# Retention with a gated MLP: the order in which the second tile's outputs and chunk 21 are made, and a queue for one early load

## Chip, cores, metric

The kernel runs on one core of one Trainium2 chip. The metric is the device time of one execution in microseconds; three runs of the kernel before gave 298.43 (median), 298.27 and 302.54. The engines are named as the profile names them: PE is TensorE, DVE is VectorE, ACT is ScalarE, POOL is GpSimd, SP is SyncE, which issues DMA transfers; PEld is TensorE's weight load.

## What is computed

The inputs are q, k and v of 8 batches, 8 heads, 576 positions and 64 columns, and two weights. Everything is given in float32.

```python
scores = (1/sqrt(64)) * q @ k.T                   # per batch and head
gamma  = 1 - 2 ** (-5 - head)
Dmat   = gamma ** (i - j) where i >= j, else 0
attn   = (scores * Dmat) @ v                      # a decaying, causal, linear attention
x      = attn with the heads side by side         # 4608 rows of 512
h      = x @ w_in                                 # 512 -> 2048
g      = h * tanh(softplus(h))                    # mish
out    = g @ w_out                                # 2048 -> 512
```

## The kernel before

**Chunks and tiles.** A chunk is 128 rows of the attention (all heads of 128 positions). There are 36. Chunks 0 to 7 are the first 128 positions of the eight batches. From chunk 8 on, two batches follow each other: three chunks each, and then one chunk that holds the last 64 positions of both. Chunk 14 is the first of these last ones, chunk 21 the second. Four chunks make a tile of 512 rows for the products of the MLP, so there are nine tiles: tile 0 is chunks 0 to 3, tile 1 is chunks 4 to 7.

**The products.** `g1(t, f)` makes 128 of the 2048 hidden columns of tile t: four matmuls of 128x512 into a bank `hp`, then mish on ScalarE into `gT`. `g2(t, i)` makes a quarter of the sum for one of the tile's four output chunks: four matmuls into a bank `ops`. The fourth quarter is followed by a copy (`res`) and a store. Both issue their matmuls in `product` (L527, or L532 where a matmul is cut in two halves of 256 columns).

**The attention of a first chunk** (tiles 0 and 1) is direct. `f_transpose` makes q and k transposed, `f_scores` the masked scores `sm0`, `f_v` the values in bf16 (`vb`), and `f_out` the outputs: eight matmuls (L249) of `vb` with `sm0` into a bank, and a copy to `xT`, the tile's input for `g1`. For tile 1 two calls share one `sc` tile, which has two banks: b = 0 and 2 take its first bank, b = 1 and 3 the second. There the copy stands behind the second call of each pair and moves both halves.

**The other chunks** keep a running state. A chunk n is loaded by POOL's queue (`load`: q and k into `qkraw`, v into `vraw`), scaled by VectorE with two instructions (`step_p`, L304, into `qks`), transposed (`step_t`: before chunk 16 on TensorE, from 16 on by a DMA transpose on SP's queue, L333, held behind a matmul, its gate), and worked on two at a time in a `visit`: states (L402), outputs (L461, L478), scores of the next two (L347), then the copies of the outputs to `xT` (L490, one on ScalarE, one on VectorE) and the masked scores `sm` (L353, VectorE). The banks of the visit's outputs are two `hp`, the same that `g1` needs next. `hold` makes POOL's queue wait for a transposed chunk before it goes on with loads.

**Order.** Everything is ordered by hand: each engine works its instructions in the order in which the program lists them, and waits at semaphores. The scheduler only places the waits. A wait is placed by tile and buffer. The stretches that matter here are:

- The start: two loads of f32 q for batches 0 and 1 into `q0` (L121, on SP's queue), loads of k, q, v and weights on POOL's queue, and VectorE's cast of `q0` to bf16 (L639).
- The loop over the 16 columns blocks i of tile 0's second product (`g2_first(i // 4, i % 4)`, L696 to L711). The table `steps` (L695) says which work of tile 1 stands ahead of which block. "V0" to "V3" are the calls of `f_v`, "O0" to "O3" those of `f_out`. The blocks 12 to 15 are the last quarters of tile 0's four output chunks, each followed by its copy and store, by VectorE for even and ScalarE for odd chunks.
- The loop from L776 on, over tiles t and steps i. n counts the chunk that is visited next, w = i % 8 the step in its eighth; the visit of n and n + 1 stands at w = 6. At w = 4 and 5 or 4 and 7 (L797) the two chunks n + 4 and n + 5 are scaled, and their transposes stand at w = 6 and 7 (L800, L826, L837 to L839). `NPE` is 18. At n = 16, w = 5, VectorE also has `f_state` (L803, the values `v0s` of a later batch).

So, before, at n = 16: chunk 20 is scaled at w = 4, chunk 21 at w = 5, the visit of 16 and 17 is at w = 6, and both transposes follow it.

Of the kernel before, what the change touches and what calls it, by code (L numbers as in the profile page):

```python
# [16 lines left out]
def kernel(  # L17
# [18 lines left out]
    nc = tc.nc  # L36
    B, H, S, D = q.shape
    assert (B, H, S, D) == (8, 8, 576, 64)
    P = 128
# [6 lines left out]
    NPE = 18  # L46
    NT = 16
# [50 lines left out]
    q0 = gts[0][:, H:nF, :].bitcast(F32).rearrange("p (b a) c -> p b (a c)", a=2)  # L98
    v0 = {}
    fst = {}  # L100
# [17 lines left out]
        nc.gpsimd.dma_start(out=pair, in_=v[ds(b, 2), :, 0:P, :].rearrange("b h p d -> p (b h) d"))  # L118

    for b in range(2):  # L120
        nc.sync.dma_start(out=q0[:, b, :], in_=q[b, :, 0:P, :].rearrange("h (g r) d -> g h (r d)", r=8))  # L121
    for b in range(2):
        load_first_qk(0, 1, b)

# [47 lines left out]
    xts = {}  # L172
# [5 lines left out]
    def f_mix(g, i):  # L178

        name = ("qb", "kb")[i]  # L180
        fst[1][name, "mix", g] = first.tile([P, 8, 2, D], BF16, name=name + "x")
        nc.vector.tensor_copy(fst[1][name, "mix", g].rearrange("p r x d -> p x r d"),
                              fst[1][name][:, ds(2 * g, 2), :].rearrange("p x (r d) -> p x r d", r=8))

    def f_transpose(t, g, i, parts):

        name = ("qb", "kb")[i]
        out_t = tr.tile([P, 2, NP, P], BF16, name="qkT", bufs=6).rearrange("p i n t -> p (i n) t")
        n = 8 // len(parts)
        moves = []  # L190
        for j, (pool, tname, copy) in enumerate(parts):
            tp = pool.tile([P, 2, 8, P] if tname == "sc" else [P, 8, P], BF16, name=tname)
            tp = (tp[:, 0] if tname == "sc" else tp)[:, 0:n]
            for r in range(n):
                if t == 1:
                    mix = fst[1][name, "mix", g][:, n * j + r]
                    nc.tensor.transpose(tp[:, r, :], mix.rearrange("p x d -> p (x d)"), ident)
                else:
                    for x in range(2):
                        nc.tensor.transpose(tp[ds(64 * x, 64), r, :],  # L200
                                            fst[0][name][:, 2 * g + x, ts(n * j + r, D)], ident)
            moves.append((copy, out_t.rearrange("p h (g r) -> p h g r", r=8)[:, :, :, ds(n * j, n)],
                          tp.rearrange("p r (g h) -> p h g r", h=H)))
        for copy, to, src in moves:
            copy(to, src)
        fst[t][name, g] = out_t
# [21 lines left out]
    def f_v(t, b, copy):  # L228
        vb = first.tile([P, H, D], BF16, name="vb", bufs=4)
        copies = copy if isinstance(copy, tuple) else (copy,)  # L230
        n = H // len(copies)
        for j, copy in enumerate(copies):
            copy(vb[:, ds(n * j, n), :], v0[4 * t + b][:, ds(n * j, n), :])
        fst[t]["vb"][b] = vb

    def f_out(t, b, copy):
        if b == 0:
            xts[t] = xp.tile([P, KC, NCH * P], BF16, name="xT")
        vb = fst[t]["vb"][b]
        if t == 0:  # L240
            pool, name = ((ps_h, "hp"), (ps_h, "hp"), (ps_st, "st"), (ps_o, "ops"))[b]
            ot = pool.tile([P, NP, P], F32, name=name)
        else:
            if b % 2 == 0:
                fst[1]["out"] = ps_sc.tile([P, 2, NP, P], F32, name="sc")
            ot = fst[1]["out"][:, b % 2]
        for p in range(NP):
            for e in range(2):
                nc.tensor.matmul(ot[ds(64 * e, 64), p, :], lhsT=vb[:, 2 * p + e, :],  # L249
                                 rhs=fst[t]["sm", b][:, 2 * p + e, :],  # L250
                                 start=(p == 0), stop=True, skip_group_check=True)
        if t == 0:
            copy(xts[t][:, :, ts(b, P)], ot)
        elif b % 2:
            copy(xts[1].rearrange("p h (b i) -> p b h i", i=P)[:, ds(b - 1, 2)], fst[1]["out"])

    def f_state(t, b, engine=nc.gpsimd):

# [187 lines left out]
    def run(jobs, *how):  # L446
        while jobs:
            jobs.pop()(*how)
# [141 lines left out]
    def g2_first(part, s):  # L590

        if part == 0:
            pool, name = ((ps_h, "hp"), (ps_h, "hp"), (ps_o, "ops"), (ps_st, "st"))[s]
            outs[0, s] = pool.tile([P, d_model], F32, name=name)
        for f in range(4 * part, 4 * part + 4):
            halved[0] = 1
            product(outs[0, s], gts[0][:, f, ts(s, P)], w_out_t[:, f, :], f == 0, f == nF - 1)
        if part == 3:
            store(0, s, outs[0, s], nc.scalar.copy if s % 2 else nc.vector.tensor_copy)
# [30 lines left out]
    dve, act, pool = nc.vector.tensor_copy, nc.scalar.copy, nc.gpsimd.tensor_copy  # L630
# [61 lines left out]
        g1(0, f)  # L692
    for i in range(2):
        f_mix(0, i)
    steps = {0: "T0", 3: "S0 C1", 9: "T1", 11: "S1", 12: "V0 V1 V2 V3", 14: "O0 O1", 15: "O2 O3"}  # L695
    for i in range(nF):  # L696
        for step in steps.get(i, "").split():
            n = int(step[1])
            if step[0] == "T":
                for j in range(2):  # L700
                    f_transpose(1, n, j, [(ps_sc, "sc", (dve, act)[j])])
            elif step[0] == "S":
                f_scores(1, n)
            elif step[0] == "V":
                f_v(1, n, dve if n == 3 else act)
            elif step[0] == "C":
                for j in range(2):
                    f_mix(n, j)
            else:
                f_out(1, n, (dve, act)[n // 2])  # L710
        g2_first(i // 4, i % 4)  # L711
    load_k0(1)

# [12 lines left out]
    for u in range(24):  # L726
        j, w = divmod(u, 4)
# [48 lines left out]
    for t in range(2, nT + 1):  # L776
        for i in range(nF):
            n, w = NCH * (t + 1) + i // 8 * 2, i % 8
            if w == 2 and n in cast_at:
                cast_k0(cast_at[n])  # L780
            if w == 2:
                run(casts, act)
                halved[0] = {14: 16, 20: 29}.get(n, 0)
            if w == 6 and n + 4 == NPE:
                load_k0(3)
            if w == 6 and n < n_chunks:
                visit(n, ((ps_h, "hp"), (ps_h, "hp")), (act, dve), lambda: g2(t - 1, i))
            if w == 0:
                stores(act if n == N0 + 4 else dve)
                run(sums)  # L790
            if w == 7 and n + 2 == NPE:
                stores()
            if w in (0, 1) and n + 2 < NT:
                att(n + 2 + w, "P")
            if w in ((3, 4) if n + 2 < NPE else (0, 1)):
                att(n + 2 + (w in (1, 4)), "V")
            if w in ((4, 7) if n + 4 <= NPE else (4, 5)) and n + 4 >= NT:  # L797
                stores()
                att(n + 4 + (w != 4), "P")
            if w == 7 and NT <= n + 4 <= NPE:  # L800
                step_t(n + 5, newest[0])
            if w == 5 and 16 <= n < 24:
                f_state(1, n // 2 - 8, nc.vector)  # L803


            if w in (1, 3) and n + 2 == NT:
                more_loads(n + 5 + w // 3, newest[0])
            if w == 1 and n + 2 == NPE:
                more_loads(n + 5, newest[0])
            if w == 1 and NPE < n + 2 < n_chunks:  # L810
                hold(n + 2)
            if w == 1 and n + 2 >= NPE:
                more_loads(n + 7)
                if t in (3, 4):
                    load_k0(2 * t - 2 + i // 8)
            if w in (4, 5) and n + 2 < NT:
                att(n - 2 + w, "T")
            stores()


            if t == 2:
                if w == 6:
                    g2(1, 8 + i // 2)
                g1(t, i)
                if w == 6:
                    step_t(n + 4, newest[0])  # L826
                if i % 2 and w != 7:
                    g2(1, 8 + i // 2)
            elif t == nT:
                if i < 12:  # L830
                    g2(t - 1, i)
            elif w == 6:

                last = n < n_chunks <= n + 2
                g2(t - 1, i + last)
                g1(t, i)
                if NPE < n + 4 < n_chunks:  # L837
                    for x in (4, 5):
                        step_t(n + x, newest[0])  # L839
            elif w == 7 and n < n_chunks <= n + 2:  # L840
                g1(t, i)
            elif i % 4 == 0:
                g1(t, i)
                g1(t, i + 1)
                g2(t - 1, i)
            else:
                if i % 4 != 1:
                    g1(t, i)
                g2(t - 1, i)
# [32 lines left out]
```

## Time and profile before

| | |
|---|---|
| median of three runs | 298.43 us |
| the profiled execution, its own time | 298.47 us |
| its span, first to last instruction | 296.8 us |
| TensorE (PE) busy | 287.3 us, 97% |
| VectorE (DVE) busy | 138.3 us, 47% |
| ScalarE (ACT) busy | 133.1 us, 45% |
| GpSimd (POOL) busy | 128.0 us, 43% |
| HBM | 38.80 MB read, 9.44 MB written |
| granted TensorE clock | 1.000 over the span |

How to read the lines. A line of the timeline has the start in us, the length in us, the engine, the line of the kernel, the operation, what it writes and reads, the shape, and the number of instructions that are merged in it; in square brackets stand the idle time ahead of it and what ended that. In a wait line, the numbers are the total in us, the number of waits and the longest. Matmuls are pipelined: the length of a row of matmuls holds the drain of the last one, so the next row can begin before it ends, and start-to-start distances are what the work costs. A DMA issue's length is that of the issuing, and the landing is later.

### The profile page before, as it was taken

To read this page: it belongs to the slowest core of one execution; us is meant where nothing else is said; L and a number is where in the kernel's file an instruction comes from. 1 tells how busy PE (TensorE), PEld (TensorE's weight loads), DVE (VectorE), ACT (ScalarE), POOL (GpSimd) and SP (SyncE) were. 2 spreads that over 40 slices of the span, in tenths; PEclk is the share of its full clock that TensorE was granted. 3 is DMA by queue.
4 is the path that set the end of the run, shared out by engine and by line. 5 is a ranking of instruction groups with operands and counts; after the bars stand their busy time and mean duration, and the time that the engine had idled before them with its cause. 6 is when DMAs were issued, how large, how long until landed. Compare 5 with 4: busy or idle time off the path is not lost.

```text
span 296.8 us, 7900 instructions
## 1 busy us (share of the span) xinstructions
PE 287.3 (97%) x3442; PEld 157.1 (53%) x3480; DVE 138.3 (47%) x251; ACT 133.1 (45%) x219; POOL 128.0 (43%) x167
## 2 busy tenths in 40 slices
PE   8899999999999999999999999999999999999996
PEld 3466887555456544457645454545454544444443
DVE  5841646697955828453546453535354222010011
ACT  4866126776665444444363435343434433433200
POOL 8845756666818195557384727283020000000000
PEclk9999999999999999999999999999999999999999
DMA  7999999999989999998979868686314110110131
GB/s 159 223 201 205 205 239 216 339 228 211 258 200 187 178 228 239 176 246 204 201 192 203 207 159 209 145 204 145 83 48 95 38 38 37 37 35 35 53 91 71
DMA packets 42275, 47.97 MB, mean 162 GB/s; under 512 B 23936, under 2 KB 31104, under 8 KB 42240
## 3 DMA queue, kind: packets, MB, share of 16 engines
q0 software_dynamic: 15440, 32.25, 51.4%
q1 hardware_dynamic: 26656, 15.01, 21.3%
q8 instruction: 27, 0.44, 0.7%
q10 hardware_dynamic: 144, 0.20, 0.2%
q14 instruction: 8, 0.07, 0.1%
HBM read 38.80 MB, written 9.44 MB: 163 GB/s over the span
## 4 chain that ended last, share of the span: by engine, by line
PE 78%; DMA 14%; POOL 4%; issue 2%; DVE 2%; DVEq 0%; POOLq 0%
PE hp L527 37%; PE ops L527 29%; DMA vpair<-in_v_dram 4%; DMA w_out_t<-in_moe_w_out_dram 4%; DMA w_in_t<-in_moe_w_in_dram 3%; DMA qkraw<-in_k_dram 2%; PE hp L532 2%; PE ops L532 2%; PE sc L347 1%; PE sc L402 1%; PE hp L478 1%; PE hp L608 1%; PE hp L461 1%; POOL gT L107 1%; PE sc L325 1%
## 5 line engine op out<-in xcount | busy, mean ns | idle before, releaser
L527 PE MATMUL hp<-xT,w_in_t 128*128 128x512 bf16 (+1 forms) x507 | 126.5, 376 | 1.2 <-DVE xT L490 0.4
L564 ACT ACTIVATE gT<-hp 128x512 bf16<-128x512 f32 x142 | 84.8, 598 | 91.1 <-PE hp L527 84.6
L527 PE MATMUL ops<-w_out_t,gT 128*128 128x512 bf16 x411 | 101.9, 379 | 2.0 <-issue 1.9
L527 PEld LDWEIGHTS <-w_in_t 128*128 128x128 bf16 x528 | 51.4, 98 | 53.9 <-issue 0.9
L527 PEld LDWEIGHTS <-gT 128*128 128x128 bf16 x478 | 45.5, 98 | 52.6 <-issue 0.6
L616 DVE COPY res<-ops 128x512 f32<-128x512 f32 x28 | 19.3, 690 | 89.5 <-PE ops L527 89.5
L304 DVE TENSOR_TENSOR qks<-qkraw,gqk 128x512 bf16<-128x512 f32 x56 | 35.3, 683 | 7.3 <-DMA qkraw<-in_k_dram 7.3
L282 POOL DMA_DIRECT2D qkraw<-in_q_dram x24 | 21.5, 896 | 14.5 <-PE hp L527 7.0
L311 POOL TENSOR_TENSOR vs<-vraw,gv 128x512 bf16<-128x512 f32 x16 | 16.4, 1044 | 17.2 <-PE hp L461 17.1
L282 POOL DMA_DIRECT2D vraw<-in_v_dram x24 | 21.4, 893 | 3.1 <-DMA vpair<-in_v_dram 1.5
L282 POOL DMA_DIRECT2D qkraw<-in_k_dram x24 | 21.2, 885 | 2.4 <-DMA qkraw<-in_q_dram 0.9
L490 DVE CAST xT<-hp 128x512 bf16<-128x512 f32 x13 | 9.0, 691 | 27.1 <-PE hp L478 27.1
L490 ACT CAST xT<-hp 128x512 bf16<-128x512 f32 x14 | 8.2, 586 | 28.5 <-PE hp L478 28.5
L532 PEld LDWEIGHTS <-gT 128*128 128x128 bf16 x164 | 15.7, 98 | 3.2
L438 DVE TENSOR_TENSOR total<-sc,total 128x256 f32<-128x256 f32 x40 | 16.9, 421 | 1.0
L496 POOL COPY held<-qkT 128x1 bf16<-128x1 bf16 x8 | 1.5, 189 | 36.6 <-DMA qkT<-qks 36.6
L353 DVE TENSOR_TENSOR sm<-sc,mask 128x1024 bf16<-128x1024 f32 x14 | 17.0, 1215 | 0.3 <-PE sc L347 0.3
L532 PE MATMUL hp<-xT,w_in_t 128*128 128x256 bf16 x102 | 15.7, 272 | 0.0
L532 PEld LDWEIGHTS <-w_in_t 128*128 128x128 bf16 x104 | 10.2, 98 | 6.8 <-issue 0.4
L441 ACT CAST ssb<-total 128x768 bf16<-128x768 f32 (+3 forms) x13 | 11.7, 896 | 1.7 <-DVE total L438 1.6
L527 PE MATMUL hp<-w_out_t,gT 128*128 128x512 bf16 x49 | 12.0, 379 | 0.2 <-issue 0.2
L532 PE MATMUL ops<-w_out_t,gT 128*128 128x256 bf16 x80 | 10.4, 273 | 0.1
(126 smaller groups left out, 251.7 us busy)
## 6 DMA issues: line engine op xcount, KB each, us to landing
out_dram<-res SPq DMA_DIRECT2D x31, 256.0 KB, 3.0
qkraw<-in_q_dram POOLq DMA_DIRECT2D x24, 256.0 KB, 6.4
qkraw<-in_k_dram POOLq DMA_DIRECT2D x24, 256.0 KB, 6.7
vraw<-in_v_dram POOLq DMA_DIRECT2D x24, 256.0 KB, 6.9
w_out_t<-in_moe_w_out_dram POOLq DMA_DIRECT2D x4, 512.0 KB, 11.8
k0r<-in_k_dram POOLq DMA_DIRECT2D x8, 256.0 KB, 7.7
gT<-in_k_dram POOLq DMA_DIRECT2D x8, 128.0 KB, 6.3
gT<-in_v_dram POOLq DMA_DIRECT2D x2, 512.0 KB, 7.4
```

Source lines behind the costliest of these rows:

```text
L107: nc.gpsimd.dma_start(out=fst[t][name][:, b, :], in_=(q, k)[i][4 * t + b, :, 0:P, :].rearrange("h (g r) d -> g h (r d)", r=8))
L282: ins = nc.gpsimd.dma_start(out=t, in_=src[b, :, ds(P * c, P), :].rearrange("h p d -> p h d"))
L304: nc.vector.tensor_tensor(slots[:, :, y], heads[:, :, y], factors[:, :, y].unsqueeze(3).to_broadcast([P, NP, 2, D]), op=OP.mult)
L311: engine.tensor_tensor(vs, live[n]["v"], gv[:, c, :].unsqueeze(2).to_broadcast([P, H, D]), op=OP.mult)
L353: nc.vector.tensor_tensor(sm.rearrange("p e x n i -> p (e x n) i"), live[n]["sc"].rearrange("p e x n i -> p (e x n) i"), mask.unsqueeze(1) ...
L438: nc.vector.tensor_tensor(new[:, k], st[:, j, x], total[b], op=OP.add)
L441: casts.append(lambda copy: copy(lows[:, 0:k], new[:, 0:k]))
L490: copy(xts[t][:, :, ds(P * s, 2 * P)].rearrange("p h (x j i) -> p j h x i", x=2, j=2)[:, j], both[j])
L527: newest[0] = nc.tensor.matmul(to, lhsT=w, rhs=x, start=first, stop=last)
L532: nc.tensor.matmul(to[:, ts(j, n)], lhsT=w, rhs=x[:, ts(j, n)], start=False, stop=False, skip_group_check=True)
L564: done = nc.scalar.activation(gts[t][:, f, :], hp, AX.Mish)
L616: copy(ot, ops)
```

## The change

Three places are changed.

1. *The second tile's outputs.* In the table, O0 and O1 move from ahead of block 14 to ahead of block 15, where O2 and O3 stand. Each call of `f_out` now ends with a copy of its own 512 columns: VectorE for b = 0 and 2, ScalarE for b = 1 and 3. Before, VectorE copied O0 and O1 in one instruction of 1024 columns, and ScalarE O2 and O3. The calls of a pair still share one `sc` tile.
2. *Chunk 21.* At n = 16, w = 4 and 7 are the steps at which the chunks n + 4 and n + 5 are scaled, so chunk 21 is scaled at w = 7, behind the visit at w = 6. Its transpose is issued at w = 7, right behind its scaling, and no longer together with that of chunk 20. On VectorE's queue the two instructions for chunk 21 move past `v0s`, a copy to `xT` and `sm`. On SP's queue the order is the same.
3. *The load of q.* The second of the two f32 loads of q is issued on ScalarE's queue, ahead of its table load, and no longer on SP's.

```diff
-        nc.sync.dma_start(out=q0[:, b, :], in_=q[b, :, 0:P, :].rearrange("h (g r) d -> g h (r d)", r=8))
+        (nc.sync, nc.scalar)[b].dma_start(out=q0[:, b, :], in_=q[b, :, 0:P, :].rearrange("h (g r) d -> g h (r d)", r=8))
...
-        if t == 0:
-            copy(xts[t][:, :, ts(b, P)], ot)
-        elif b % 2:
-            copy(xts[1].rearrange("p h (b i) -> p b h i", i=P)[:, ds(b - 1, 2)], fst[1]["out"])
+        copy(xts[t][:, :, ts(b, P)], ot)
...
-    steps = {0: "T0", 3: "S0 C1", 9: "T1", 11: "S1", 12: "V0 V1 V2 V3", 14: "O0 O1", 15: "O2 O3"}
+    steps = {0: "T0", 3: "S0 C1", 9: "T1", 11: "S1", 12: "V0 V1 V2 V3", 15: "O0 O1 O2 O3"}
...
-                f_out(1, n, (dve, act)[n // 2])
+                f_out(1, n, (dve, act)[n % 2])
...
-            if w in ((4, 7) if n + 4 <= NPE else (4, 5)) and n + 4 >= NT:
+            if w in ((4, 7) if n + 4 <= NPE + 2 else (4, 5)) and n + 4 >= NT:
                 stores()
                 att(n + 4 + (w != 4), "P")
-            if w == 7 and NT <= n + 4 <= NPE:
+            if w == 7 and NT <= n + 4 <= NPE + 2:
                 step_t(n + 5, newest[0])
...
                 if NPE < n + 4 < n_chunks:
-                    for x in (4, 5):
+                    for x in ((4, 5) if n + 4 > NPE + 2 else (4,)):
                         step_t(n + x, newest[0])
```

Lines of the changed kernel are three lower from L255 on, and the copy of `f_out` is its L252.

## The prediction

> **What bounds the kernel now.** I read the page first, then TensorE's waits, then two stretches of the timeline: 43 to 50 us, where the second tile's outputs are made, and 111 to 117 us, where chunk 21 is scaled. From the page:
>
> ```profile
> span 296.8 us, 7900 instructions
> PE 287.3 (97%) x3442; PEld 157.1 (53%) x3480; DVE 138.3 (47%) x251; ACT 133.1 (45%) x219; POOL 128.0 (43%) x167
> ...
> PE 78%; DMA 14%; POOL 4%; issue 2%; DVE 2%; DVEq 0%; POOLq 0%
> ```
>
> TensorE (PE) is busy for 97% of the span and is 78% of the chain that ended last. DMA is 14% of that chain, all but 2% of it before 45.4 us (the weights, then `vpair`); after that the chain is TensorE alone but for one place. So there is almost no idle time in which a later loss could be made good, and every idle moment that a change puts on TensorE is paid in full. Of TensorE's waits, only one after 13 us is not "issue":
>
> ```profile
> PE hp L527 <- DVE xT L490: 0.4, 1, 0.4
> ```
>
> The columns are the total, the number and the longest. The timeline of TensorE and VectorE (DVE) shows where that one is:
>
> ```profile
> 112.76 1.03 PE L527 MATMUL hp<-xT,w_in_t 128*128 128x512 bf16 x4
> 114.17 1.02 PE L527 MATMUL hp<-xT,w_in_t 128*128 128x512 bf16 x4 [0.38 <-DVE xT L490]
> ```
> ```profile
> 111.62 1.29 DVE L304 TENSOR_TENSOR qks<-qkraw,gqk 128x512 bf16<-128x512 f32 x2 [2.58 <-DMA qkraw<-in_k_dram]
> 112.83 0.68 DVE L261 TENSOR_TENSOR v0s<-vpair,gv 128x512 bf16<-128x512 f32 x1
> 113.44 0.68 DVE L490 CAST xT<-hp 128x512 bf16<-128x512 f32 x1
> 114.04 1.21 DVE L353 TENSOR_TENSOR sm<-sc,mask 128x1024 bf16<-128x1024 f32 x1
> 116.09 0.69 DVE L616 COPY res<-ops 128x512 f32<-128x512 f32 x1 [0.84 <-PE ops L527]
> ```
>
> VectorE's queue stood 2.58 us at the scaling of chunk 21 (L304) for its rows of k, and `xT`, a copy of the visit of 16 and 17 that frees the bank for the next product, was behind it. The visit's last matmuls end near 111.9.
>
> The other stretch, timeline of 43.5 to 50 us (O0 to O3 are the calls of `f_out` for the second tile, L249):
>
> ```profile
> 44.69 0.64 PE L249 MATMUL sc<-sm,vb 128*64 128x128 bf16 x16
> ...
> 45.26 0.83 PE L532 MATMUL ops<-w_out_t,gT 128*128 128x256 bf16 x6
> ...
> 45.48 0.43 DVE L233 CAST vb<-vpair 128x512 bf16<-128x512 f32 x1 [1.06 <-DMA vpair<-in_v_dram]
> ...
> 45.83 0.68 DVE L616 COPY res<-hp 128x512 f32<-128x512 f32 x1
> ...
> 46.24 0.64 PE L249 MATMUL sc<-sm,vb 128*64 128x128 bf16 x16
> 46.43 1.21 DVE L255 CAST xT<-sc 128x1024 bf16<-128x1024 f32 x1
> ...
> 46.81 0.83 PE L532 MATMUL st<-w_out_t,gT 128*128 128x256 bf16 x6
> ...
> 46.92 1.01 ACT L255 CAST xT<-sc 128x1024 bf16<-128x1024 f32 x1 [0.37 <-PE sc L249]
> ...
> 47.69 1.25 PE L527 MATMUL hp<-xT,w_in_t 128*128 128x256 bf16 x9
> ```
>
> O0 with O1, a quarter of a product, O2 with O3, another quarter: the two copies run while TensorE does the quarters. From 44.69 to the second tile's first product at 47.69 it spends 3.00 us, of which its own work needs 2.88: two pairs at 0.57 (44.69 to 45.26) and two quarters at 0.87 (the same eight 256-column matmuls go by 0.87 at 36.06, 36.94, 37.81, 38.68).
>
> **The change, part by part.**
>
> *Outputs in one place, copied by two engines.* The quarter that stood between the pairs moves ahead of O0, and each 1024-wide copy becomes two of 512: O0 and O2 on VectorE, O1 and O3 on ScalarE (ACT). TensorE's work is the same 2.88 us. What is new lies in the waits of the built program. O0 and O1 write two halves of one tile (two banks of one `sc`), and so do O2 and O3. Before, the copy came after both halves were written. Now the copy of O0 stands between the two, and the first matmul of O1 waits for VectorE's count 64, which is the copy of O0; the first of O3 waits for 65, the copy of O2. So the four outputs run one behind another through VectorE, and TensorE, which works in order, idles in between. Step by step, from 44.69, where neither order waits:
>
> - quarter 44.69 to 45.56 (0.87); O0 45.56 to 45.85 (half of 0.57), results out near 46.0.
> - VectorE, in order: `vb` at 45.48 (when `vpair` lands), the copy of `hp` at 45.83, then the copy of `ops`, which now precedes O0's copy, at 46.43 (0.60 later, as 45.83 to 46.43 shows), then O0's copy from 47.03. A 512-wide copy out of PSUM to bf16 takes 0.69 (the page's groups have `L253 DVE CAST xT<-ops` at 691 ns), so it ends at 47.72.
> - O1 starts at 47.77 (0.05 from VectorE's end to TensorE's start, as 47.64 to 47.69). Idle: 47.77 - 45.85 = 1.92 us.
> - O1 to 48.05, O2 (its `vb` is ready at 46.06) to 48.34, results near 48.48; O2's copy 48.52 to 49.21; O3 starts at 49.26. Idle: 0.92 us.
> - O3 to 49.54, the last quarter to 50.41. O1's copy on ScalarE ends near 48.8, O3's near 50.3 (0.59 each), both ahead of the product. The second tile starts at 50.41 and not at 47.69: **+2.72 us**.
>
> Bounds: if `vpair` lands 0.7 us earlier, O0's copy is held only by the `ops` copy (that quarter is out near 45.74) and the term falls to about 2.0; if both of VectorE's copies start 0.4 us behind their matmuls (the idle time that the page has before the copies of L253), it rises to 3.5. If the wait were met early, -0.12 (2.88 against 3.00). What is late next: VectorE's scaling of chunk 8 goes from 48.16 to about 49.1, but TensorE reaches its transposes 2.7 us later too (50.40 to 53.1), so that stays hidden. SP's stores of these tiles and POOL's loads wait on copies that are at most some 2 us later; their data is not wanted for many us.
>
> *Chunk 21 behind the visit.* Its two scaling instructions (1.29 us) go from before `v0s` and `xT` to after `sm`. VectorE is then free when the visit ends: `xT` 111.95 to 112.6, `sm` to 113.8, chunk 21 to 115.0; the copy at 116.09 waits for TensorE anyhow and has 0.84 us of cover. TensorE's four matmuls at 112.76 would be followed after 0.86, not 1.41: **-0.55 us** (the row's idle time is 0.38 because a matmul's modelled end includes its drain). The transpose of 21 keeps its place on SP's queue behind that of 20, and its gate is the same matmul. Bound: if it starts late, nothing is hurt up to the next visit's scores at 126.88; from 115.2 it landed in 7.5 us, at 122.7, so 4.2 us are spare (SP's timeline, below). The gain lies between 0 (the bank is waited for otherwise) and 0.55.
>
> ```profile
> 115.20 5.48 SPq L333 DMA_TRANSPOSE qkT<-qks  x1
> ```
>
> *Second f32 q on ScalarE's queue.* The issue (0.57 to 0.70 us on SP) moves ahead of ScalarE's table load, behind which it idled 2.78 us. The half lands near 5.9 (issued 1.57, 4.3 to landing), and VectorE, busy without a gap, casts it at 6.4. It may land 0.7 us earlier and no one waits for it. Bounds: -0.2 (DMA is short of full only in its first us, and could start the long stream to `vpair` so much earlier) to +0.3 (it shares with the k rows that TensorE transposes at 6.49). I take 0.
>
> **Sum.** 2.72 - 0.55 + 0 = +2.17 us. The profiled execution took 298.47 (span 296.8 and 1.67 around it), 0.04 from the median 298.43 of the runs. 298.47 + 2.17 = 300.64, so 300.6.
>
> **Rivals.**
>
> *The pause slows TensorE's clock.* At the start, from rest, matmuls of 512 columns stand 0.43 us apart for 5 us, and later 0.216:
>
> ```profile
> 1.26 5.30 PE L170 MATMUL ops<-zeros 128*128 128x512 bf16 x12 [1.26 <-DVE pos L135]
> ```
>
> The two pauses leave 0.57 us of work in 3.4 us. If the slow state came back for as long as at the start, half of 5.2 us would be lost: +2.6, so 303.2. Against it: TensorE's waits of 0.19, 0.53 and 0.27 us between 10.5 and 12.6 did not bring it back (379 ns per matmul at 13.2).
> The Trainium skill ("TensorE: Matmul & The Clock Gate", Part 1) says that the clock halves after at least one idle window of about 3.4 us; by that page neither pause (1.92, 0.92) is one, and if the window did count as idle, an estimate from it is half a window, +1.7. The trace agrees so far as its short pauses go; none of 3.4 us is in it.
>
> *The other side: the waits cost nothing.* Place: O1's first matmul. If the copy of O0 were done when TensorE gets there, the part gives -0.12, chunk 21 -0.55: 297.8. It decides if O0's copy ends before 45.9. For it: single copies of 512 are shorter than 1024. Against it: VectorE is at `vb` until 45.83 because of `vpair`, with two copies in front.
>
> *One pause only.* If `vpair` lands early or O3's wait is met, about 1.8 or 2.0 instead of 2.72: 299.7 to 299.9.
>
> *A loss given back later.* For it: less DMA pressure, as loads not gated by TensorE come 2.7 us earlier against it. Against it: TensorE's other waits after 48 us are 12 "issue" gaps of 0.2 at most, 1.9 in all. At best half: 299.7.
>
> *The transpose of 21 late* for the scores at 126.88: it takes over 4.2 us; each us beyond is one more, so about 301.6.
>
> **How the numbers follow.** Forecast 0.68; one pause or given back 0.13; clock 0.07; other side 0.06; late transpose 0.03; others 0.03. The forecast's own range is 299.9 to 301.5 (the bounds of the first term, and 0 to 0.55 for the second). Reaching into the cases of one pause and of the clock, the range is 299.3 to 302.2. Two per cent, about what a measurement tells from no change, is 6 us: above 304.4 or below 292.5. No case but the clock's with something on top gets there: slower 0.03, faster 0.01, same 0.96.
>
> **What would show it.** Right: TensorE waits of 1.5 to 2.2 us and 0.7 to 1.2 us at the L252 copies' releases, the first product of the second tile near 50.4, and no 0.38 us wait for `xT` near 116. Wrong: O1 following O0 without a pause; the product's start before 49; matmuls 0.43 apart after 50; a wait for a transposed chunk near 129; or a TensorE that stands again as early as before at 110 us.

## The result, and the profile after

The changed kernel took 301.43 us (median of 22 executions), the kernel before 298.4 on the same chip. The ratio is 1.0092, 95% interval 1.0075 to 1.011: slower by some 2.75 us. It leaves out the executions of the kernel before that are over 1.5% above its fastest (302.5 to 303.9 us). The forecast was 300.6, range 299.3 to 302.2.

The profiled execution took 300.28 us. Its page:

```profile
span 298.5 us, 7902 instructions
PE 287.0 (96%) x3442; PEld 157.5 (53%) x3480; DVE 138.7 (46%) x252; ACT 133.3 (45%) x220; POOL 129.4 (43%) x167
```

TensorE (PE) is as busy as before (287.0 against 287.3 us), and the span is 1.7 us longer: the time is in waits. TensorE's waits name them (total, number, longest):

```profile
PE sc L249 <- DVE xT L252: 1.8, 2, 1.0
...
PE hp L536 <- DMA w_in_t<-in_moe_w_in_dram: 1.2, 1, 1.2
```

The first line is the pair of waits that the prediction put there. The second was not predicted. The wait for `xT` in a visit is gone. The timeline of the stretch with the outputs:

```profile
45.60 0.43 DVE L233 CAST vb<-vpair 128x512 bf16<-128x512 f32 x1 [0.22 <-DMA vpair<-in_v_dram]
...
46.51 0.41 PE L249 MATMUL sc<-sm,vb 128*64 128x128 bf16 x8
46.61 0.69 DVE L613 COPY res<-ops 128x512 f32<-128x512 f32 x1
...
47.22 0.68 DVE L252 CAST xT<-sc 128x512 bf16<-128x512 f32 x1
47.95 0.64 PE L249 MATMUL sc<-sm,vb 128*64 128x128 bf16 x16 [1.03 <-DVE xT L252]
...
48.63 0.69 DVE L252 CAST xT<-sc 128x512 bf16<-128x512 f32 x1 [0.73 <-PE sc L249]
...
49.37 0.41 PE L249 MATMUL sc<-sm,vb 128*64 128x128 bf16 x8 [0.78 <-DVE xT L252]
...
50.60 1.25 PE L524 MATMUL hp<-xT,w_in_t 128*128 128x256 bf16 x9
```

O0 (eight matmuls at 46.51), VectorE's copy of it at 47.22, only then O1 with O2 (sixteen at 47.95), the copy of O2 at 48.63, only then O3 at 49.37. The second tile starts at 50.60 and not at 47.69.

Chunk 21, in the timelines of TensorE, VectorE and GpSimd:

```profile
115.08 1.89 PE L524 MATMUL hp<-xT,w_in_t 128*128 128x512 bf16 x8
```
```profile
114.19 0.69 DVE L487 CAST xT<-hp 128x512 bf16<-128x512 f32 x1 [2.22 <-PE hp L475]
...
115.93 2.13 DVE L301 TENSOR_TENSOR qks<-qkraw,gqk 128x512 bf16<-128x512 f32 x2
```
```profile
115.95 3.01 POOL L308 TENSOR_TENSOR vs<-vraw,gv 128x512 bf16<-128x512 f32 x2
```

The eight matmuls run through, where before four and four stood apart. The scaling takes 2.13 us, not 1.29.

### The profile page after: what moved, and what is told of

It is laid out like the page before. It is cut to its first block, busy times and chain, and to the rows that moved or that the text cites. A ratio compares the mean times of both kernels' runs of the same rounds, so it can differ in the third digit from the quotient of the medians.

```text
span 298.5 us, 7902 instructions
## 1 busy us (share of the span) xinstructions
PE 287.0 (96%) x3442; PEld 157.5 (53%) x3480; DVE 138.7 (46%) x252; ACT 133.3 (45%) x220; POOL 129.4 (43%) x167
## 4 chain that ended last, share of the span: by engine, by line
PE 79%; DMA 15%; POOL 3%; issue 2%; DVE 1%; POOLq 0%; DVEq 0%
PE hp L524 37%; PE ops L524 30%; DMA vpair<-in_v_dram 4%; DMA w_out_t<-in_moe_w_out_dram 4%; DMA w_in_t<-in_moe_w_in_dram 3%; DMA qkraw<-in_k_dram 3%; PE ops L529 2%; PE hp L529 1%; PE sc L344 1%; PE sc L399 1%; PE hp L475 1%; PE hp L458 1%; PE hp L605 1%; POOL gT L107 1%; POOL w_in_t L87 1%
## 5 line engine op out<-in xcount | busy, mean ns | idle before, releaser
L301 DVE TENSOR_TENSOR qks<-qkraw,gqk 128x512 bf16<-128x512 f32 x56 | 36.1, 697 | 3.0 <-DMA qkraw<-in_k_dram 3.0
L308 POOL TENSOR_TENSOR vs<-vraw,gv 128x512 bf16<-128x512 f32 x16 | 17.3, 1104 | 17.5 <-PE hp L458 17.4
```

Of the source, the lines that this page charges most:

```text
L301: nc.vector.tensor_tensor(slots[:, :, y], heads[:, :, y], factors[:, :, y].unsqueeze(3).to_broadcast([P, NP, 2, D]), op=OP.mult)
L308: engine.tensor_tensor(vs, live[n]["v"], gv[:, c, :].unsqueeze(2).to_broadcast([P, H, D]), op=OP.mult)
```

## The experiments

Three theories were at hand. A: O1 and O3 wait for VectorE's copies, because both halves of a pair are one tile. B: part of the loss is at the start, where `w_in` came late, because of the new place of the q load. C: the pauses take TensorE's clock down; 12 of the 22 executions of the changed kernel had a mean granted clock of 0.993 to 0.994 and took 301.88 us on average, the other 10 had 1.000 and took 300.18. Some executions of the kernel before show 0.994 too (7 of 35 beside the first experiments). They are some 4 us longer than its others, and no trace shows where their clock falls, so what follows on the clock is about the changed kernel alone.

**The outputs alone**, on the kernel before:

```diff
-        if t == 0:
-            copy(xts[t][:, :, ts(b, P)], ot)
-        elif b % 2:
-            copy(xts[1].rearrange("p h (b i) -> p b h i", i=P)[:, ds(b - 1, 2)], fst[1]["out"])
+        copy(xts[t][:, :, ts(b, P)], ot)
...
-    ... 14: "O0 O1", 15: "O2 O3"}
+    ... 15: "O0 O1 O2 O3"}
...
-                f_out(1, n, (dve, act)[n // 2])
+                f_out(1, n, (dve, act)[n % 2])
```

> The kernel before with the second tile's outputs alone changed. Theory A (O1 and O3 wait for VectorE's copies of O0 and O2, as both halves are one tile): two TensorE pauses, 1.9 and 0.9 us, and the first product of the second tile 2.7 us later than 47.69, if TensorE reaches O0 as early as before (45.85 at the end of O0); with a start that is later for another reason the first pause shrinks by as much. Time +1.8 to +2.7 us against before. Theory B (the time went to the start, where w_in landed at 16.2 and not 15.0 us because of the q load on ScalarE's queue): +1 us or less here, and no 1.2 us wait for w_in at 16 us in either. Theory C (the pauses halve TensorE's clock for a window in some executions): a part of the executions has a mean clock near 0.994 and is some 1.7 us longer than the others.

Measured: 300.58 us, ratio 1.0081 (1.0047 to 1.0115). TensorE's waits:

```profile
PE sc L249 <- DVE xT L252: 3.1, 2, 2.3
```

The pauses are 2.31 and 0.78 us: `vpair` landed 0.4 us later in this execution and TensorE came 0.3 us earlier than in that of before, so the first one is longer than the 1.92 forecast. The first product starts at 50.77, 3.08 us late. There is no wait for `w_in`. Eight executions at full clock (0.999 or 1.000) lie between 299.9 and 301.1, and four at 0.988 to 0.994 between 301.2 and 302.8. So this part by itself makes nearly the whole loss. Full clock against full clock it is 2.0 us (300.28 on average against 298.28 of 28 executions of the kernel before). The share below full clock is one third here and not one half, though the pauses are longer in this profile.

**The q load alone:**

```diff
-        nc.sync.dma_start(out=q0[:, b, :], ...)
+        (nc.sync, nc.scalar)[b].dma_start(out=q0[:, b, :], ...)
```

> The kernel before with the second f32 q on ScalarE's queue alone. Theory B (the load's place makes w_in land later): a TensorE wait for w_in of about 1.2 us near 16 us, and +0.6 to +1.2 us in time. Rival (the late w_in of the one profile was chance): no such wait, time within 0.3 us of before, perhaps 0.2 us less as the transposes start 0.2 us earlier. Theory C: no pauses at 46 to 49 us, so the mean clock stays 1.000 unless the wait for w_in alone brings it down.

Measured: 298.28 us, ratio 0.9988 (0.9947 to 1.003), and no wait for `w_in` in its profile: the first piece landed 7.2 us after its issue (7.5 before, 8.7 in the changed kernel). Theory B falls. The next kernel settles it from the other side.

**Chunk 21 alone** (the three conditions with `NPE`, as in the change):

> The kernel before with chunk 21 scaled and transposed behind the visit, alone. Expected by the prediction's second term: the four matmuls at 112.76 are followed after 0.86 and not 1.41 us, no wait for xT there, -0.55 us in time (297.9 against 298.4). Rival (chunk 21's transpose lands late or its scaling delays the copy at 116): 0 or more.

Measured: 297.99 us, ratio 0.9993 (0.9962 to 1.0023). Its profile has no wait for `xT` in a visit, as expected. It has the wait for `w_in`, though q is loaded as before:

```profile
PE hp L539 <- DMA w_in_t<-in_moe_w_in_dram: 1.1, 1, 1.1
```

So a late `w_in` comes with either place of the q load (8.5 us to landing here, 7.8 in a second profile of the changed kernel, which has no such wait). And the gain of 0.55 us is not one that each execution has to give: the two kernels above scale chunk 21 in the old place, and their profiles have no wait of 0.38 us there; the kernel with the q load alone runs its eight matmuls through:

```profile
112.72 1.89 PE L527 MATMUL hp<-xT,w_in_t 128*128 128x512 bf16 x8
```

Its k rows had let the scaling begin at 111.00, not at 111.62, and `xT` came in time.

**A bank for each output**, on the changed kernel, with the copies where they are:

```diff
-            if b % 2 == 0:
-                fst[1]["out"] = ps_sc.tile([P, 2, NP, P], F32, name="sc")
-            ot = fst[1]["out"][:, b % 2]
+            if b < 2:
+                ot = ps_sc.tile([P, 2, NP, P], F32, name="sc")[:, 0]
+            else:
+                ot = ps_h.tile([P, NP, P], F32, name="hp")
```

> The changed kernel with a bank of its own for each of the four outputs (two in sc tiles, two in hp), the copies at the same places of the program and on the same engines. Theory A: the two pauses go; the first product of the second tile is within 0.4 us of where TensorE's own work would put it (2.88 us after the quarter's start), and the time is 1.8 to 2.5 us below the changed kernel's. Rival (the four copies themselves, or their place behind two copies to res, hold TensorE): pauses of 0.7 us and more stay. Theory C: with the pauses the executions at a clock near 0.994 go too, which takes off about 0.9 us more on average.

Measured: 298.28 us, ratio to before 1.0017 (0.9982 to 1.0052). TensorE's timeline:

```profile
45.89 0.64 PE L250 MATMUL sc<-sm,vb 128*64 128x128 bf16 x16
46.64 0.64 PE L250 MATMUL hp<-sm,vb 128*64 128x128 bf16 x16
47.21 0.83 PE L530 MATMUL st<-w_out_t,gT 128*128 128x256 bf16 x6
48.09 1.25 PE L525 MATMUL hp<-xT,w_in_t 128*128 128x256 bf16 x9
```

The four outputs follow each other. From the quarter's start (44.93) to the first product it is 3.16 us, 0.28 above TensorE's own 2.88. Engines, copies and order are those of the changed kernel and only the tiles differ, so theory A is shown: what cost the time is one tile for two outputs with a copy between them. Theory C's part came true only in part: 10 of the 12 executions are at full clock, but two are still at 0.994 (301.3 and 301.7 us). With no such pause in this kernel, something else can take the clock down too; no trace shows what.

**The changed kernel again:**

> The changed kernel once more, unaltered, beside the next three and on their chip. Theory C (the pauses near 48 us take TensorE's clock down for some 3.5 us in a part of the executions): about half of the executions at a mean clock near 0.994, as 12 of 22 were, and those 1.7 us longer; a profile of such an execution shows matmuls of 512 columns 0.43 us apart somewhere between 46 and 56 us. Rival (the lower clock comes from elsewhere, as 7 of 35 executions of the kernel before also had it): a share near one fifth, or slow matmuls in another place.

Measured: 301.4 us, ratio 1.0094 (1.007 to 1.0117), three of six executions at 0.994 (301.86 on average; the others 300.8). The distance is 1.05 us here, from three executions each, where 1.7 was expected. The profiled execution is one at 0.994. The view by stretches has the length, the busy time of PE, PEld, DVE, ACT and POOL (with instruction counts), the granted clock of TensorE, the DMA share and GB/s:

```profile
45.99:49.40 3.41, 1.23 (x30) 0.93 (x31) 2.68 (x6) 1.24 (x3) 2.40 (x3) 1.00 1.03 216
49.40:52.81 3.41, 3.41 (x22) 2.21 (x20) 1.68 (x4) 1.17 (x2) 2.64 (x3) 0.50 1.02 226
```

and the timeline of TensorE:

```profile
47.85 0.64 PE L249 MATMUL sc<-sm,vb 128*64 128x128 bf16 x16 [1.40 <-DVE xT L252]
49.27 0.56 PE L249 MATMUL sc<-sm,vb 128*64 128x128 bf16 x8 [0.78 <-DVE xT L252]
49.76 1.46 PE L529 MATMUL st<-w_out_t,gT 128*128 128x256 bf16 x6
...
51.44 1.93 PE L524 MATMUL hp<-xT,w_in_t 128*128 128x256 bf16 x9
```

The clock falls to a half right behind the pauses, for 3.41 us, and comes back. The quarter of 0.87 us takes 1.68 (49.76 to 51.44). Half of 3.41 us is 1.7 us, and the mean clock is 1 - 1.7/300 = 0.994.

**Work in the pauses:**

```diff
         copy(xts[t][:, :, ts(b, P)], ot)
+        if t == 1 and b % 2 == 0:
+            keep_warm((4, 3)[b // 2], ps_h, "hp")
```

> The changed kernel with four matmuls of zeros (512 columns) between O0 and O1 and three between O2 and O3, into a free bank, so that TensorE works while it waits for the copies; the results are as before. Theory C: the share of executions at 0.994 falls to that of the kernel before (about one fifth) or to none, and the time of the others stays within 0.4 us of the changed kernel's at full clock (300.2). Rival: the share stays at about one half.

Measured: all five executions at 1.000, but 301.73 us, ratio 1.0105 (1.0084 to 1.0126). On average the five are 0.75 us above the three of the changed kernel at full clock beside them, so the time did not stay within the 0.4 us expected. Its profile has a stop of TensorE of 1.1 us near 105 us, where no semaphore is waited for, and none of the others has one of that size there. Hence a second kernel, with three and two of them in place of four and three:

> The changed kernel with three and two matmuls of zeros in the two pauses instead of four and three. Theory C: again no execution at 0.994, or one in five at most. On the time, two readings of the kernel with four and three (all at full clock, yet 301.6): if its 1.1 us stop of TensorE near 105 us, where no semaphore is waited for, comes with the added instructions, it is here again and the time is near 301.5; if it was chance, the time is 300.2 to 300.8.

Measured: 300.64 us, ratio 1.009 (1.0056 to 1.0123); six of six at 0.999 or 1.000. With both, none of 11 executions is at 0.994, against 15 of 28 of the changed kernel. Five of the six lie between 300.3 and 301.2; the profiled one, at 302.23, again has two stops of 0.7 and 0.5 us with no semaphore, elsewhere. Why these stops come is open. The traces give a hint that no run tested: in the DMA records each of the three ends 1.4 to 1.5 us behind the end of a transfer of 16 KB of instructions (the stop of 1.1 us at 106.43, the transfer at 104.93).

**The pause doubled:**

```diff
-        copy(xts[t][:, :, ts(b, P)], ot)
+        for _ in range(3 if t == 1 and b == 0 else 1):
+            copy(xts[t][:, :, ts(b, P)], ot)
```

> The changed kernel with VectorE's copy of O0 done three times instead of once (the same values to the same place), which puts two copies of 0.60 us ahead of O1 and doubles the first pause. Theory A: the first pause grows by 1.2 us and the first product of the second tile starts as much later; at equal clock the time is 1.0 to 1.2 us above the changed kernel's (300.2 at full clock), so 301.2 to 301.5. Theory C: with a nearly idle stretch of some 4.8 us and not 3.6, every stretch of 3.4 us finds place in it, so nearly all executions have a mean clock of 0.994 or less and a median near 303. Rival: the share at 0.994 stays near one half, the median between 301.3 and 302.5.

Measured: 303.13 us, ratio 1.0165 (1.013 to 1.02); all six executions between 0.988 and 0.994. The first pause is 2.88 us. Against the changed kernel's executions at 0.994 (301.86) the five at 0.993 or 0.994 are 1.1 us longer (302.96): the two added copies, as theory A has it. The stretches show the half clock:

```profile
48.00:52.00 4.00, 2.19 (x31) 1.55 (x31) 3.24 (x6) 1.17 (x2) 3.02 (x4) 0.92 1.03 215
52.00:56.00 4.00, 4.00 (x22) 2.63 (x21) 2.38 (x5) 1.78 (x3) 2.97 (x5) 0.66 1.05 346
```

For the changed kernel theory C is shown from three sides: the fall is seen in a trace, it is gone when the pauses are filled, and it is there each time when they are longer.

**Without the outputs' change** (chunk 21 and q together):

> The changed kernel without the change of the outputs: chunk 21 behind the visit and q on ScalarE's queue. Theory A: all of the loss is gone; 297.8 to 298.4 us, the same as before or up to 0.6 us below it. Rival (the parts hurt together): above 299.

Measured: 298.05 us, ratio 0.9994 (0.9979 to 1.0009). It beats the changed kernel (301.4 us beside it), and no measurement here tells it from the kernel before. All twelve executions are at 0.999 or 1.000.

**The copies of a pair behind both outputs**, still one tile:

```diff
-        copy(xts[t][:, :, ts(b, P)], ot)
+        if t == 0:
+            copy(xts[t][:, :, ts(b, P)], ot)
+        elif b % 2:
+            for e, one in enumerate((dve, act)):
+                copy_to = xts[1][:, :, ts(b - 1 + e, P)]
+                one(copy_to, fst[1]["out"][:, e])
```

> The changed kernel with the copies of a pair behind both of its outputs (so that no matmul waits for a copy), still one tile for a pair, VectorE for the even and ScalarE for the odd one. Theory A (the order that one tile forces): no TensorE pause ahead of O1 or O3, but ScalarE's copy waits for VectorE's of the same tile, so the first product of the second tile starts 0.3 to 0.9 us later than with a bank each; time 298.5 to 299.3. Rival (only matmuls behind copies matter): as with a bank each, 298.3.

Measured: 298.51 us, ratio 0.9999 (0.9984 to 1.0014). The 32 matmuls of the four outputs run in one stretch, and one wait is left, for ScalarE's copy, which had waited for VectorE's of the same tile:

```profile
48.42 1.41 PE L529 MATMUL hp<-xT,w_in_t 128*128 128x256 bf16 x9 [0.60 <-ACT xT L257]
```

3.63 us from the quarter's start (44.79), 0.47 more than with a bank each. The mechanism is as theory A has it; in time it is too small to be told from nothing. Three of the twelve executions are at 0.989 to 0.994, though no matmul waits for a copy between the outputs, and they take 303 to 304 us, like those of the kernel before.

## Why the prediction was right, point by point

**The outputs, +2.72: right in kind.** The two pauses are where they were put, and the experiment with a bank each shows the cause. The size hangs on when `vpair` lands against TensorE's arrival: in the profile after, TensorE came 0.85 us later than before (the quarter at 45.54 and not at 44.69, from the wait for `w_in`) while `vpair` landed only 0.1 us later, so the first pause was 1.03 and not 1.92 us (0.12 of the difference is the drain of the matmuls ahead, which the profile counts as work and the prediction did not). From quarter to first product it is 5.06 us, 2.06 above the 3.00 of before. With the outputs alone it is 6.34 (44.43 to 50.77), 3.34 above. Both lie within the bounds given, 2.0 to 3.5, but the upper one for another reason than the prediction's: no copy of VectorE's started 0.4 us late there; `vpair` landed later and TensorE came earlier.

**Chunk 21, -0.55: over-sized.** At its place the profile after shows 0.54: the lag of each matmul behind its time before falls from 2.32 to 1.77 us at 114 us. But that wait belonged to one execution; it is missing in two other profiles with the old place, and alone the part gives 0.9993 with an interval of 0.0061, which holds 0 as well as -0.55. The prediction took one execution's DMA landing for the kernel's. It also took 1.29 us for the scaling behind the visit; there it runs beside GpSimd's scaling of v and takes 2.13 (2.99 and 2.82 in the profiles of the kernel without the outputs' change and of the one with the copies behind both outputs), while GpSimd's two go from 2.05 to 3.01. In the profile after this cost nothing, since the copy behind it moved only to 117.98 and TensorE waits for none of it.
The Trainium skill ("SBUF — State Buffer", Who interferes with whom) says that a VectorE instruction with two SBUF inputs contends with a GpSimd instruction that reads SBUF, and that the later one blocks until the other is done. The trace agrees: the pairs get longer by 0.84 and 0.96 us where they overlap, and of VectorE's two multiplications the first took 0.68 us and the second, which came behind GpSimd's first, 1.53.

**The q load, 0: right.** 0.9988 alone, with 0 well inside the interval.

**"A loss given back later" came true in part.** The profile after starts the second tile 2.91 us late and ends 1.7 late. Of the difference, 0.54 is chunk 21, and some 0.6 are two short stops of the execution before, with no semaphore waited for, that the one after does not have: the lag falls by 0.34 us at 72.8 and by 0.25 at 104.4. That is chance of the two executions; no run shows it to belong to the kernels.

**The other rivals** did not come: both pauses are there, O0's copy ends at 47.90 and not before 45.9, and TensorE waits for no transposed chunk near 129 us.

**The clock: the rival of 0.07 came true in about half of the executions.** This is the step that failed. At full clock the changed kernel takes 300.18 us, where the sum said 300.64; the 12 of 22 executions with a lower clock take 1.7 us more, and the median is at 301.43. So the sum was 0.5 us too high for the one kind and 1.2 too low for the other, and that the median still lies in the range is in part luck: its upper end had been reached out toward this rival. Two things were wrong in the reasoning. Against it stood short waits of 0.2 to 0.5 us at the start, which say nothing of two pauses close together. And its price was taken from the cold start, 2.6 us; a window's is 1.7, as the estimate beside it from the Trainium skill's page had it ("TensorE: Matmul & The Clock Gate", Part 1). By the words of that page of the Trainium skill the clock halves after an idle window of about 3.4 us, and the prediction read it as a stretch without any work. The trace has 3.41 us for the window, but TensorE was busy in 1.23 of the 3.41 us ahead of the fall, so it need not be idle.

How much work is too little also depends on where the stretch lies. The profile of the outputs alone is at full clock, though TensorE is busy there for just 0.64 of the 3.41 us from 46.00 to 49.41. In the clock records of the traces, the changes of the clock in one execution are a whole number of stretches of 3.413 us apart (in the second profile of the changed kernel they are at 5.02, 49.40 and 52.81 us, 13 stretches and one), and this grid lies at another place in each execution. In the profile of the outputs alone it cuts the pauses in two (first two lines); in that of the doubled pause the stretch ahead of the fall is the third line:

```profile
44.24:47.65 3.41, 1.57 (x18) 0.97 (x16) 1.82 (x5) 1.10 (x2) 1.31 (x2) 1.00 1.06 225
47.65:51.06 3.41, 2.10 (x33) 1.71 (x34) 2.68 (x5) 1.26 (x3) 2.42 (x4) 1.00 1.03 215
```
```profile
47.93:51.34 3.41, 1.52 (x29) 1.24 (x29) 2.65 (x5) 1.02 (x2) 2.43 (x3) 1.00 1.04 216
```

A fall came after 1.23 and after 1.52 us of work in a stretch of the grid, and none after 1.57 and more; with the pauses filled no stretch, wherever it is laid, has less than 2.05. So the same pauses can bring the fall in one execution and not in the next. These are five profiles, with busy times that the profile estimates; no run was made to find the limit.

## What to carry to other kernels

Before a copy is split for two engines, look at what the waits are placed by: here two halves of one tile count as one thing, so a copy between the two writes makes the second write wait, and two copies of it wait for each other; a tile for each output removed all but 0.28 us of it. On an engine that is busy for 97% of the span, add up the pauses over a stretch of 3.4 us and not one by one: here none is that long, and together they cost another 1.7 us in each execution in which the clock follows them. And a wait seen in one profile is worth its price only if it is there in a second one.

## What the runs showed of the hardware that was not expected

- TensorE's granted clock went to 0.50 for 3.41 us after a stretch of 3.41 us in which it was busy for 36%. The mean clock was 0.994 or less in 15 of 28 executions of the changed kernel (1.8 and 2.2 us of pauses in its two profiles), in 4 of 12 of the outputs alone (3.1), in six of six with the pause doubled (3.7), and in none of 11 with the pauses filled.
- In the eleven traces that record changes of the granted clock, they lie a whole number of 3.413 us apart, and where this grid lies differs: the first change is between 3.9 and 7.1 us after the first instruction.
- The first piece of `w_in`, issued at 7.5 to 7.6 us, landed 7.2 to 8.7 us later in different executions with the same loads issued ahead of it on its queue, and TensorE waited for it 1.1 to 1.2 us or not at all.
- Two VectorE multiplications beside two of GpSimd took 2.13 and 3.01 us in the profile after, and 1.29 and 2.05 apart in the one before.
